# Maxima of the first eight attention units computed between the projections, by sums and differences of key blocks

## The chip, the cores and the metric

The kernel runs on one core of a Trainium2 chip. The metric is the device time of one execution in microseconds (us), lower is better. The core's engines are TensorE (PE, the matmuls), VectorE (DVE), ScalarE (ACT), GpSimd (POOL), and SyncE (SP), whose queue issues the DMAs.

## The reference

One transformer block with adaptive layer norm, all in float32, on 2048 rows of 512 numbers, with 32 heads of 16 and an inner width of 1792:

```python
mod = (silu(c) @ w_mod).reshape(1, 6, 1, 512)
sa, ca, ga, sb, cb, gb = (mod[:, i] for i in range(6))
h = layernorm(x) * (1 + ca) + sa
q, k, v = split(h @ wqkv)                  # 32 heads of 16
p = softmax(q @ k.T / 4)                   # 2048 x 2048 for each head
x = x + ga * ((p @ v) @ wo)
h = layernorm(x) * (1 + cb) + sb
out = x + gb * (gelu(h @ w1 + b1) @ w2 + b2)
```

The softmax needs, for each head and each query row, the largest of 2048 scores before the exponentials are taken.

## The kernel before

The work has three stages: the projections, the attention and the feed-forward part. Products that need more precision than one pass gives are split into a high and a low half, so a product of 512 terms is 12 matmuls of 128x512 (`mm3`, its matmuls on line 274): this is called an item here.

**Projections.** A loop over four blocks `b` of 512 rows normalizes and transposes the block, and computes k and q of the first quarter of the heads (`proj_qk(b, 0, 1)` and `proj_qk(b, 0, 0)`) and four items of v (`proj_v`). Then 24 items follow: k and q of the other three quarters. k and q go to DRAM in their split form (line 297) and are read back in the layout that the attention wants (`build_k`, `build_q`); v goes to DRAM too (line 317) and comes back as `vg` (line 500).

**Attention.** The work is cut into 32 units: a group `g` of four heads (8 groups) times a block `qb` of 512 queries (4 blocks). A unit has 16 steps, one for each 128 keys; there are 512 steps. A step computes four score tiles of 128 keys x 512 queries (`exp_step`: the matmul on line 735 into a bank of the pool `sc`, the exponential by ACT on line 736), named X0 to X3, and one burst P (`pv_step`, line 571), which multiplies the exponentials of the step before with v for the four heads. The four heads of a group lie as two planes `p` and two row halves `a`: heads with a=0 use rows 0 to 49 of PE's array, heads with a=1 rows 64 to 113. So X0 and X2 are in half 0, X1 and X3 in half 1.

**Maxima.** The maxima of a unit are taken before its exponentials and enter the score matmul as two extra rows of the query operand. A unit has 64 banks of them: 128 queries x 512 keys, for 2 planes, 2 halves `a`, 4 query chunks and 4 key blocks (`max_bank`, matmul on line 382). A bank of half 0 is reduced by DVE (line 391). In half 1 two of the four key blocks are reduced like that, and two go by their sum and difference, because max(x, y) = (x+y)/2 + |x-y|/2: the keys' sums and differences were formed in the projections (`pm`, `pmh`, lines 289 to 301, stored as `kpm`), the difference bank goes through |.| on ACT (line 385, in a bank of the pool `sc`), and one DVE instruction (line 388) adds the sum bank and reduces. `max_rows` collects a unit's maxima, transposes them on PE (line 402) and sends them by way of DRAM into the query tile. `next_max(a)` does the next bank of a half; the tokens M0 and M1 stand for it.

The order of a step is written out by hand:

```python
ORDER = ("X0 X1 X2 M1 M0 X3 P".split(), "X0 M1 X1 X2 M1 M0 X3 P M1 M0 M0".split())
```

for even and odd steps: two and six banks, four on average. 83 banks (`LEAD`) are taken ahead, between the matmuls of the last 21 items, four at a time; such a group of banks in an item is called a visit here. PSUM has eight banks: three for maxima (`ps_mx`), four for scores and items (`ps_sc`), one for P (`ps_pv`).

**What sets the order.** Each engine takes its instructions in program order, and a buffer or bank is reused in a ring, so that a matmul that writes a bank waits for the instruction that read it last. SP issues all DMAs in one queue, in order. The hooks (`at`) place side work into steps: output projections of the first query block in the last unit (lines 720 to 725), loads of later groups (lines 741 and 757 to 763).

**Feed-forward.** Line 781 and after; the change does not touch it but for the buffers it inherits.

Of the kernel before, what the change touches and what calls it, by code (L numbers as in the profile page):

```python
# [16 lines left out]
P = 128  # L17
S = 2048
# [16 lines left out]
FILL0 = 3  # L35
LEAD = 2 * NM + 19
# [5 lines left out]
ORDER = ("X0 X1 X2 M1 M0 X3 P".split(), "X0 M1 X1 X2 M1 M0 X3 P M1 M0 M0".split())  # L42
ORDER_END = "X0 X1 P X2 X3".split()
# [4 lines left out]
def block_kernel(ctx: ExitStack, tc: tile.TileContext, x, wqkv, wo, w1, b1, w2, b2, c, w_mod, out):  # L48
# [12 lines left out]
    ps_mx = ctx.enter_context(tc.tile_pool(name="ps_mx", bufs=3, space=PSUM))  # L61
    ps_sc = ctx.enter_context(tc.tile_pool(name="ps_sc", bufs=4, space=PSUM))
    ps_pv = ctx.enter_context(tc.tile_pool(name="ps_pv", bufs=1, space=PSUM))

    def bank_mx():
        return ps_mx.tile([P, TB], F32, tag="mx", name="mx")

    def bank():
        return ps_sc.tile([P, TB], F32, tag="sc", name="sc")

    def bank_pv():
        return ps_pv.tile([P, TB], F32, tag="pv", name="pv")
# [3 lines left out]
    kpm_d = [dram.tile([2, 2, P, TB], F32, name=f"kpm{k}") for k in range(4)]  # L76
# [23 lines left out]
    halves = [[lend.tile([P, 4, D], F32, name=f"{n}{i}") for i in range(2)] for n in ("xin", "wmod")]  # L100

# [6 lines left out]
    c_c = vwpool.tile([P, KC], F32, name="c_c")  # L108
    s_c = vwpool.tile([P, KC], F32, name="s_c")
    s_m = vwpool.tile([P, 2, KC, 32], F32, name="s_m")  # L110
    gp.memset(s_m, 0.0)
    sel = vwpool.tile([P, 32], F32, name="sel")
    sel_b = vwpool.tile([P, 2, P], F32, name="sel_b")
    ones = vwpool.tile([P, 2 * S // P], F32, name="ones")
    gp.memset(ones, 1.0)
    vslots = [vwpool.tile([P, KC, D], FR, name=f"wv{i}") for i in range(2)]
    vraw = vwpool.tile([P, KC, D], F32, name="vraw")
    vst = [vwpool.tile([P, NG, 4, VG], F32, name=f"vst{i}") for i in range(2)]
# [74 lines left out]
    def mod_copy(ps):  # L193
        r = tpool.tile([P, D], F32, tag="h32", name="mrow", bufs=3)
        ac.activation(r, ps, AF.Copy)
        return r
# [61 lines left out]
    def ln1_t(b, tiles, between=lambda: None):  # L258
        hi = hpool.tile([P, KC, TB], FR, name=f"hThi{b}")
        lo = hpool.tile([P, KC, TB], FR, name=f"hTlo{b}")  # L260
        hT[b] = hi, lo
        tr, evac = transposed(tiles, hi, lo, 0, tpool, lambda fc: bank_mx() if fc < KC - 1 else bank(), (ve, gp))
        pss = [tr(fc) for fc in range(KC - 1)]
        between()
        pss.append(tr(KC - 1))
        return lambda: [evac(fc, pss[fc]) for fc in range(KC)]
# [11 lines left out]
    def proj_qk(b, k, w, fill=()):  # L278
# [7 lines left out]
        if w and b == 2:  # L286
            k2[k] = tpool.tile([P, TB], F32, tag="k2", name="k2", bufs=1)
            ac.activation(k2[k], ps, AF.Copy)
        if w and b == 3:
            pm = [tpool.tile([P, TB], F32, tag="h32", name="pm", bufs=3) for _ in range(2)]  # L290
            pmh = [tpool.tile([P, 2, TB], FR, tag="parts", name="pmh", bufs=3) for _ in range(2)]
            for i, op in enumerate((ALU.add, ALU.subtract)):
                ve.tensor_tensor(pm[i], ps, k2[k], op=op)
                ac.activation(pmh[i][:, 0], pm[i], AF.Copy)

        def rest():
            sy.dma_start(qk_d[w][k][:, :, b * TB : (b + 1) * TB].rearrange("a p t -> p a t"), parts.bitcast(F32))
            if w and b == 3:
                for i in range(2):
                    gp.tensor_tensor(pmh[i][:, 1], pm[i], pmh[i][:, 0].bitcast(F32), op=ALU.subtract)  # L300
                    sy.dma_start(kpm_d[k][i].rearrange("a p t -> p a t"), pmh[i].bitcast(F32))
# [3 lines left out]
    def proj_v(b, t):  # L305
# [4 lines left out]
            [w_hi[4][:, i] for i in range(KC)], [w_lo[4][:, i] for i in range(KC)], late_b=False)  # L310
        v = vst[b % 2]
        ac.activation(v[:, :, t, : 4 * VW].rearrange("p g (j e) -> p g j e", e=VW)[:, :, :, :DH],
                      ps.rearrange("p (g j d) -> p g j d", j=4, d=DH), AF.Copy)

    def store_v(b):
        for g in (0, 4):
            sy.dma_start(v_d[g : g + 4, :, b * 4 : b * 4 + 4, :].rearrange("g p k e -> p g k e"),
                         vst[b % 2][:, g : g + 4])
# [3 lines left out]
    kst, kpm, qst = {}, {}, {}  # L322

    def heads(w, g, part, a, t0, t1):
        r0 = (g % 2) * 64
        ap = qk_d[w][g // 2][part, r0 : r0 + 64, t0:t1]
        return ap.rearrange("(p a d) t -> a d p t", a=2, d=DH)[a]

    def build_k(g, t0=0, t1=S):
        for i, part in enumerate((0, 0, 1)):  # L330
            for a in range(2):
                r0 = a * 64 + i * DH
                sy.dma_start(kst[g][r0 : r0 + DH, :, t0:t1].bitcast(F32), heads(1, g, part, a, t0, t1))

    def build_pm(g):

        r0 = (g % 2) * 64
        for i, part in enumerate((0, 0, 1)):
            for w in range(2):
                src = kpm_d[g // 2][w, part, r0 : r0 + 64, :].rearrange("(p a d) t -> a d p t", a=2, d=DH)[1]  # L340
                d0 = 64 + i * DH
                sy.dma_start(kpm[g][d0 : d0 + DH, :, w].bitcast(F32), src)

    def build_q(u):
        g, qb = divmod(u, NB)
        qst[u] = kqpool.tile([P, 2, TB], FR, tag="qst", name="qst", bufs=3)
        for i, part in enumerate((0, 1, 0)):
            for a in range(2):
                r0 = a * 64 + i * DH
                sy.dma_start(qst[u][r0 : r0 + DH].bitcast(F32), heads(0, g, part, a, qb * TB, (qb + 1) * TB))  # L350
# [6 lines left out]
    mx0, mx1, left, vabs = {}, {}, {}, {}  # L357

    mi = [0, 0]

    def max_bank(u, i, a, spare):

        if u not in left:
            mx0[u] = small.tile([P, 2, 4, 4], F32, tag="mx0", name="mx0")
            mx1[u] = small.tile([P, 2, 4, 3], F32, tag="mx1", name="mx1")
            left[u] = 2 * NM
        g = u // NB  # L370
        p, qc, kr = i // 16, (i // 4) % 4, i % 4
        r0 = a * 64
        rows = slice(r0, r0 + KR)
        q = qst[u][rows, p, qc * P : (qc + 1) * P]
        diff, both = a == 1 and kr == 0, a == 1 and kr == 3
        ps = bank() if diff or spare else bank_mx()
        if diff or both:
            k = kpm[g][rows, p, int(diff)]
        else:
            kr -= a  # L380
            k = kst[g][rows, p, kr * TB : (kr + 1) * TB]
        te.matmul(ps, q, k, start=True, stop=True)  # L382
        if diff:
            vabs[u, p, qc] = cpool.tile([P, TB], F32, tag="cp", name="cp")
            ac.activation(vabs[u, p, qc], ps, AF.Abs)  # L385
        elif both:
            v = vabs.pop((u, p, qc))
            ve.tensor_tensor_reduce(v, ps, v, -0.5, 3.0e38, ALU.add, ALU.min, mx1[u][:, p, qc, 2:3])  # L388
        else:
            m = mx1[u][:, p, qc, kr : kr + 1] if a else mx0[u][:, p, qc, kr : kr + 1]  # L390
            ve.tensor_reduce(m, ps, axis=AX.X, op=ALU.max, negate=True)  # L391
        left[u] -= 1

    def max_rows(u):

        mn = small.tile([P, 2, 2, 4], F32, tag="mn", name="mn")
        for a, m in enumerate((mx0.pop(u), mx1.pop(u))):
            ve.tensor_reduce(mn[:, :, a], m, axis=AX.X, op=ALU.min)

        def rest():  # L400
            ps = bank()
# [7 lines left out]
            src = m_d[u].rearrange("s (p a c) q -> a s p (c q)", a=2, c=4)  # L409
            for a in range(2):  # L410
                r0 = a * 64 + KR
                sy.dma_start(qst[u][r0 : r0 + 2].bitcast(F32), src[a])
# [3 lines left out]
    def next_max(a, spare=False):  # L416

        u, i = divmod(mi[a], NM)
        if u == NG * NB:
            return []  # L420
        mi[a] += 1
        max_bank(u, i, a, spare)
# [8 lines left out]
    for t in vst:  # L431
        gp.memset(t[:, :, :, 4 * VW :], 0.0)
        for j in range(4):
            gp.memset(t[:, :, :, j * VW + DH], 1.0)
# [17 lines left out]
    mrow = None  # L452
    for b in range(NB):
        if b == NB - 1:
            close(lcm)
            kqcm, kqpool = pool("kqpool")
            kst[0] = kqpool.tile([P, 2, S], FR, name="kst0")
            kpm[0] = kqpool.tile([P, 2, 2, TB], FR, name="kpm0")
            one_rows(kst[0])
            build_k(0, 0, b * TB)  # L460
            build_q(0)
            build_q(1)
# [9 lines left out]
        if b == NB - 1:  # L472
            build_k(0, b * TB, S)
            build_pm(0)
        if b in (1, 2):
            mrow = mod_rows(wms)
        if b:
            store_v(b - 1)
        proj_v(b, 0)
        if b + 1 < NB:  # L480
            ev = ln1_t(b + 1, xn)
            ev()
        proj_v(b, 1)
# [5 lines left out]
        proj_v(b, 2)  # L489
        proj_v(b, 3)  # L490

    store_v(NB - 1)
    close(vwcm)
    rcm, rpool = pool("rpool", bufs=2)
    cpool = rpool
    vg = {}

    def load_v(g):
        vg[g] = rpool.tile([P, NKC, VG], F32, tag="vg", name="vg")
        sy.dma_start(vg[g], v_d[g])  # L500

    items = [(b, k, w) for k in range(1, 4) for b in range(NB) for w in (1, 0)]
    todo, rest = [], None
    led = 0
    for n, (b, k, w) in enumerate(items):
        if n == 6:
            load_v(0)
        if b == 1 and w and k < 3:
# [3 lines left out]
        fill, new = [], []  # L512
        if rest:
            fill.append(rest)
        m = n + 1 - FILL0

        ms = range(led, min(LEAD, 4 * max(m, 0)))
        fill.append(lambda ms=ms: [new.extend(next_max(i % 2, i % 4 == 3)) for i in ms])
        led += len(ms)
        rest = proj_qk(b, k, w, fill)  # L520
# [3 lines left out]
    rest()  # L524
    close(wcm)
    close(hcm)
    close(tcm)

# [373 lines left out]
```

## Time and profile before

| what | value |
|---|---|
| three runs | 1823.42 us median (1819.85 to 1823.84) |
| the profiled execution | 1823.15 us, its span 1820.9 us |
| granted PE clock, mean | 0.993 |
| loop over b and items of v and first k, q | up to 103.49 us |
| 24 items with 83 banks of maxima, up to the first P | 103.49 to 198.15 us |
| attention, units 0 to 29 | 198.15 to 1379.97 us |
| attention, units 30 and 31 | 36.41 and 41.47 us |
| output projection and feed-forward | 1457.85 to 1820.9 us |

Times inside the execution are counted from the span's start. Busy time of PE is a poor measure of how full it is, since matmuls overlap in the records: one of 512 columns is shown 0.39 to 0.5 us long, while the next one starts 0.23 us after it. So the text below reads starts, not lengths. "PEld" is the loading of the stationary operand. A DMA's line is that of its issue on SP.

### The profile page before, as it was taken

The page shows a single profiled execution, that of the slowest core. Times are in us where ns is not written, and L with a number is a line of the kernel's source. Part 1 is how long each engine was busy: PE and PEld are TensorE (multiplying, and loading weights), DVE is VectorE, ACT ScalarE, POOL GpSimd, SP SyncE. Part 2 cuts the span into 40 slices and gives each one's busy share as a digit, 9 for nine tenths or more (in the row PEclk, how much of TensorE's full clock was granted, in tenths as well). Part 3 has the DMA queues.
Part 4 walks back from the last instruction along what each step waited for, and adds up shares of the span by engine and source line. Part 5 has one row for each costly group of instructions (what it writes and reads, how often), then busy time and mean ns, then how long its engine had stood idle before and what let it go on. Part 6 is the DMA issues. An engine that isn't in the chain of part 4 may idle for free.

```text
span 1820.9 us, 29277 instructions
## 1 busy us (share of the span) xinstructions
PE 1771.5 (97%) x10586; PEld 915.7 (50%) x10586; DVE 1440.5 (79%) x2627; ACT 1337.1 (73%) x2558; POOL 262.1 (14%) x258
## 2 busy tenths in 40 slices
PE   8999999999999999999999999999999999999998
PEld 6776433333333333333333333333333377788887
DVE  6347899989999999998999999899998287737453
ACT  2322799999999999998999999999999732222222
POOL 3111001000000000000000000000002044545462
PEclk8999999999999999999999999999999999999999
DMA  7774611130040122004002100400012054423341
GB/s 254 195 250 180 150 32 28 39 55 14 13 72 14 25 43 43 14 14 72 16 23 51 35 14 14 72 23 16 13 57 83 30 167 140 127 71 109 104 122 47
DMA packets 97960, 129.33 MB, mean 71 GB/s; under 512 B 14152, under 2 KB 53064, under 8 KB 96456
## 3 DMA queue, kind: packets, MB, share of 16 engines
q1 hardware_dynamic: 97816, 127.47, 27.0%
q8 instruction: 83, 1.36, 0.3%
q14 instruction: 61, 0.50, 0.1%
HBM read 91.56 MB, written 35.86 MB: 70 GB/s over the span
## 4 chain that ended last, share of the span: by engine, by line
PE 73%; DVE 15%; DMA 6%; issue 3%; SPq 2%; ACT 1%; POOL 1%; POOLq 0%; DVEq 0%; ACTq 0%
PE pv L571 25%; PE sc L735 12%; PE sc L274 10%; DVE mx L391 10%; PE mx L382 10%; PE mx L802 5%; PE sc L382 5%; DMA kst<-qk 2%; PE pv L802 2%; DMA kpm<-kpm 2%; PE sc L675 1%; DVE cp L388 1%; ACT p L736 1%; DMA qk<-parts 1%; PE mx L675 1%
## 5 line engine op out<-in xcount | busy, mean ns | idle before, releaser
L736 ACT ACTIVATE p<-sc 128x512 f32<-128x512 f32 x2048 | 1060.0, 612 | 58.6 <-PE mx L382 33.3
L391 DVE TENSOR_REDUCE mx<-mx 128x1 f32<-128x512 f32 x1526 | 981.7, 685 | 126.8 <-PE mx L382 94.8
L382 PE MATMUL mx<-kst,qst 48*128 48x512 f32 x1526 | 610.1, 454 | 28.3 <-DVE mx L391 0.4
L735 PE MATMUL sc<-qst,kst 50*128 50x512 f32 x2048 | 633.1, 422 | 1.9 <-ACT p L736 0.9
L571 PE MATMUL pv<-p,vg 128*32 128x512 f32 x4096 | 551.7, 606 | 0.0
L735 PEld LDWEIGHTS sc<-qst,kst 50*128 50x128 f32 x2048 | 309.9, 186 | 233.8 <-ACT p L736 196.3
L382 PEld LDWEIGHTS mx<-kst,qst 48*128 48x128 f32 x1526 | 258.2, 184 | 139.4 <-DVE mx L391 131.9
L781 ACT ACTIVATE g<-sc,b_c 128x512 f32<-128x512 f32 x56 | 38.6, 689 | 240.6 <-PE sc L274 236.5
L385 ACT ACTIVATE cp<-sc 128x512 f32<-128x512 f32 x256 | 153.7, 600 | 34.9 <-PE sc L382 14.4
L388 DVE CUSTOM_DVE_ANT_0 cp<-mx,cp 128x512 f32<-128x512 f32 x246 | 167.5, 681 | 0.3 <-PE sc L735 0.2
L406 POOL CAST m<-mr 16x128 fp32r<-16x128 f32 x32 | 9.1, 286 | 1084.0 <-DVE mr L404 1084.0
L571 PEld LDWEIGHTS pv<-p,vg 128*32 128x32 f32 x4096 | 81.9, 108 | 158.5 <-issue 143.2
L382 PEld LDWEIGHTS sc<-kpm,qst 48*128 48x128 f32 x266 | 48.6, 183 | 208.8 <-ACT p L736 208.8
L785 DVE TENSOR_TENSOR glo<-g,ghi 128x512 fp32r<-128x512 f32 x56 | 59.0, 1054 | 97.2 <-ACT ghi L784 97.1
L382 PE MATMUL sc<-kpm,qst 48*128 48x512 f32 x266 | 131.2, 493 | 2.6 <-DMA qst<-qk 2.6
L607 POOL TENSOR_TENSOR w1l<-w1r,w1h 128x512 fp32r<-128x512 f32 x56 | 76.5, 1366 | 152.7 <-DVE w1h L606 135.1
L382 PE MATMUL mx<-kpm,qst 48*128 48x512 f32 x246 | 97.5, 396 | 0.0
L609 POOL TENSOR_TENSOR w2l<-w2r,w2h 128x512 fp32r<-128x512 f32 x56 | 81.6, 1457 | 6.9 <-DVE w2h L608 6.5
L274 PE MATMUL sc<-p,w1h 128*128 128x512 f32 x224 | 75.0, 396 | 0.0
L274 PE MATMUL sc<-hThi,w 128*128 128x512 f32 x256 | 69.1, 413 | 4.0 <-DVE hThi L242 1.9
L802 PE MATMUL mx<-w2h,glo 128*128 128x512 f32 x168 | 66.2, 394 | 2.7 <-DVE glo L785 2.6
L802 PE MATMUL mx<-w2l,ghi 128*128 128x512 f32 x168 | 65.9, 392 | 0.0
(148 smaller groups left out, 1516.5 us busy)
## 6 DMA issues: line engine op xcount, KB each, us to landing
qk<-parts SPq DMA_DIRECT2D x32, 512.0 KB
w1r<-in_B_w_dram SPq DMA_DIRECT2D x56, 256.0 KB
w2r<-in_B_w_dram SPq DMA_DIRECT2D x56, 256.0 KB
qst<-qk SPq DMA_DIRECT2D x192, 64.0 KB
kst<-qk SPq DMA_DIRECT2D x42, 256.0 KB
wmod<-in_w_mod_dram SPq DMA_DIRECT2D x6, 1024.0 KB
v<-vst SPq DMA_DIRECT2D x8, 664.0 KB
vg<-v SPq DMA_DIRECT2D x8, 664.0 KB
```

What stands on the lines that cost most here:

```text
L274: te.matmul(ps, p, q, start=i == 0, stop=i == len(terms) - 1)
L382: te.matmul(ps, q, k, start=True, stop=True)
L385: ac.activation(vabs[u, p, qc], ps, AF.Abs)
L388: ve.tensor_tensor_reduce(v, ps, v, -0.5, 3.0e38, ALU.add, ALU.min, mx1[u][:, p, qc, 2:3])
L391: ve.tensor_reduce(m, ps, axis=AX.X, op=ALU.max, negate=True)
L571: te.matmul(cur_pv[0][32 * j : 32 * (j + 1)], vg[g][:, kc, j * VW : j * VW + 32], pt.pop((s, j)), start=kc == 0, stop=kc == NKC - 1)
L607: gp.tensor_tensor(alo, a, ahi.bitcast(F32), op=ALU.subtract)
L609: gp.tensor_tensor(blo, b, bhi.bitcast(F32), op=ALU.subtract)
L735: te.matmul(ps, k[r0 : r0 + KX, p, kc * P : (kc + 1) * P], q[r0 : r0 + KX, p], start=True, stop=True)
L736: ac.activation(pb, ps, AF.Exp, scale=SCALE)
L785: ve.tensor_tensor(glo, g, ghi.bitcast(F32), op=ALU.subtract)
L802: te.matmul(acc[qb][t], p[:, sl], q, start=f == 0 and n == 0, stop=f == NF - 1 and n == 2)
```

## The change

All 64 banks of units 0 to 7 (the first two head groups) move between the projections, where four visits of four banks stand in each item (`VISIT`, `FILL0`); each visit holds a pair of difference banks and a pair of sum banks, and a unit's maxima are now all taken by sums and differences of key blocks, block 2r with 2r+1. Sums and differences are formed for the first quarter of the heads alone, now for blocks b=1 and b=3. Eight of the sixteen v items move from the loop over b into the filled part. For that part PSUM is divided into two banks for items and six for maxima, and afterwards as before. What the visits in the items do not hold is done behind the last item.

In the attention, only units 8 to 31 are left: all their banks are plain, with DVE's reduction, and no bank of maxima uses the pool of scores. A step has three banks where it had four, and some steps one more (`EXTRA`). Queries for maxima and for exponentials are loaded into tiles of their own (`qmx`, `qst`), and the keys of a group are loaded a group earlier. The output projections of the first query block are placed in four single steps.

```diff
-FILL0 = 3
-LEAD = 2 * NM + 19
+NU1 = 8
+FILL0 = 2
+VISIT = 2
...
-ORDER = ("X0 X1 X2 M1 M0 X3 P".split(), "X0 M1 X1 X2 M1 M0 X3 P M1 M0 M0".split())
+ORDER = ("X0 X1 M0 X2 M0 X3 P M1".split(), "X0 X1 M1 X2 M1 X3 P M0".split())
+
+EXTRA = {5: 0, 13: 1, 17: 1, 25: 0}
+ORDER_END = "X0 X1 X2 X3 P".split()
...
+    def pair_slot(kind, n):
+        u, i = divmod(n, 16)
...
+        p, qc, r = i // 8, (i // 2) % 4, i % 2
+        t0 = (2 * r + (kind == "V")) * TB
+        pss = [bank_mx() for _ in range(2)]
+        for a, ps in enumerate(pss):
+            rows = slice(a * 64, a * 64 + KR)
+            te.matmul(ps, qmx[u][rows, p, qc * P : (qc + 1) * P], kpm[u // NB][rows, p, t0 : t0 + TB],
+                      start=True, stop=True)
+        if kind == "V" and i == 2:
+            load_qm(u + 1)
+        if kind == "V":
+            for a, ps in enumerate(pss):
+                vabs[n, a] = tpool.tile([P, TB], F32, tag="cp", name="cp", bufs=6)
+                ac.activation(vabs[n, a], ps, AF.Abs)
+            return []
+        for a, ps in enumerate(pss):
+            v = vabs.pop((n, a))
+            ve.tensor_tensor_reduce(v, ps, v, -0.5, 3.0e38, ALU.add, ALU.min, mxs[u][:, p, a, qc, r : r + 1])
...
+    close(acm)
+    open_psum(sc=2, mx=6)
...
+    items = [(None, b, t) for b, t in vitems] + [(k, b, w) for k in range(1, 4) for b in range(NB) for w in (1, 0)]
+    slots = [("V", 0), ("V", 1)]
+    for n in range(2, 16 * NU1):
+        slots += [("V", n), ("U", n - 2)]
+    slots += [("U", 16 * NU1 - n) for n in (2, 1)]
...
+    def visit():
+        nonlocal led
+        for sl in slots[led : led + VISIT]:
+            new.extend(pair_slot(*sl))
+        led += VISIT
...
+        if n >= FILL0:
+            fill = [lambda rest=rest: (rest(), visit()), visit, visit, visit]
+        rest = proj_qk(b, k, w, fill) if k else proj_v(b, w, fill)
...
     rest()
+    while led < len(slots):
+        new = []
+        visit()
+        todo += new
...
+    open_psum(mx=3, sc=4, pv=1)
...
+    for t, n in enumerate((base - 2, base + 3, base + 7, base + 11)):
         for i in range(12):
-            at(base + OP0 + (12 * t + i) // OPN, lambda t=t, i=i: run(("o", t), lambda: o_proj(0, t), i))
...
+            at(n, lambda t=t, i=i: run(("o", t), lambda: o_proj(0, t), i))
...
-        if kc == 2 and u + 2 < NU:
-            build_q(u + 2)
+        if kc == 2 and 0 < u < NU - 1:
+            load_q(u + 1)
...
+        order = ORDER[s % 2] + [f"M{a}" for k, a in EXTRA.items() if k % 16 == kc and (k < 16 or u < 4)]
...
-            if g:
-                kst[g + 1] = kst[g - 1]
-                build_k(g + 1)
-                kpm[g + 1] = kpm[g - 1]
-                build_pm(g + 1)
+            if g and g + 3 < NG:
+                load_k(g + 3, kst[g - 1])
```

287 lines of the change are left out of this document (151 added, 136 removed).

## The prediction

> **What bounds the kernel now.** I read the busy shares first, then the timeline of TensorE (PE) in two attention steps, then the same in the projections. The busy shares name a candidate and no more:
>
> ```profile
> span 1820.9 us, 29277 instructions
> ...
> PE 1771.5 (97%) x10586; PEld 915.7 (50%) x10586; DVE 1440.5 (79%) x2627; ACT 1337.1 (73%) x2558; POOL 262.1 (14%) x258
> ```
>
> The timeline (start, length, engine, line, tile, count) shows what a step is made of. Between two bursts of P·V (L571) stand matmuls on 48 or 50 rows: the exp scores (L735) and the maxima (L382). They use one half of the array's rows each, a=0 or a=1, as the code sets.
>
> ```profile
> 801.14 0.49 PE L735 MATMUL sc<-qst,kst 50*128 50x512 f32 x1
> 801.15 0.49 PE L382 MATMUL mx<-kst,qst 48*128 48x512 f32 x1
> 801.48 0.39 PE L735 MATMUL sc<-qst,kst 50*128 50x512 f32 x2
> 801.71 0.39 PE L382 MATMUL mx<-kpm,qst 48*128 48x512 f32 x1
> 801.71 0.40 PE L382 MATMUL mx<-kst,qst 48*128 48x512 f32 x1
> 801.95 0.40 PE L735 MATMUL sc<-qst,kst 50*128 50x512 f32 x1
> 802.27 1.07 PE L571 MATMUL pv<-p,vg 128*32 128x512 f32 x8
> 803.27 0.50 PE L382 MATMUL sc<-kpm,qst 48*128 48x512 f32 x1
> 803.27 0.73 PE L382 MATMUL mx<-kst,qst 48*128 48x512 f32 x2
> 803.62 0.63 PE L735 MATMUL sc<-qst,kst 50*128 50x512 f32 x2
> 803.85 0.44 PE L382 MATMUL mx<-kst,qst 48*128 48x512 f32 x1
> 804.09 0.39 PE L735 MATMUL sc<-qst,kst 50*128 50x512 f32 x1
> 804.59 0.49 PE L382 MATMUL mx<-kst,qst 48*128 48x512 f32 x1
> 804.59 0.49 PE L735 MATMUL sc<-qst,kst 50*128 50x512 f32 x1
> 805.01 1.06 PE L571 MATMUL pv<-p,vg 128*32 128x512 f32 x8
> ```
>
> Matmuls of different halves start together (801.14 and 801.15); those of one half follow each other. So an interval between bursts costs **slots**: as many as the fuller half has matmuls. The first slot lasts 0.34 us (801.14 to 801.48), a later one 0.234, the last 0.326 up to the burst (801.95 to 802.27), the burst 1.00 (802.27 to 803.27). The first interval has four slots: 0.34+2x0.234+0.326+1.00 = 2.13. The second has five in half a=0 (M0 M0 X0 X2 M0): 2.37 by the same sum, but takes 2.74, since its last M0 waits until 804.59. The waits name VectorE (DVE): the ring of maxima has three banks, four M fall into this interval, and the fourth needs the first one's reduction (start 803.85, 0.69 long). The pair is 4.87 us, a unit of 16 steps about 39.2. DVE works 7 x 0.60 of those 4.87 us, ScalarE (ACT) 8 exps at 0.478 and one Abs at 0.49: neither fills it.
>
> The projections, as items of 12 full matmuls (L274), without and with one visit of four maxima banks:
>
> ```profile
> 103.49 1.98 PE L274 MATMUL sc<-hThi,w 128*128 128x512 f32 x8
> ...
> 106.21 1.98 PE L274 MATMUL sc<-hThi,w 128*128 128x512 f32 x8
> ...
> 128.63 0.73 PE L382 MATMUL mx<-kst,qst 48*128 48x512 f32 x3
> ...
> 129.30 2.10 PE L274 MATMUL sc<-hThi,w 128*128 128x512 f32 x8
> 131.24 1.07 PE L274 MATMUL sc<-hTlo,w 128*128 128x512 f32 x4
> 132.23 0.50 PE L382 MATMUL mx<-kst,qst 48*128 48x512 f32 x1
> ```
>
> An item without a visit is 106.21-103.49 = 2.72 us. From visit to visit it is 132.23-128.63 = 3.60. **A visit costs 0.88 us**: two slots and the change of shape before and after them. Here too PE is the bound.
>
> **The change, part by part.** Own time 1823.15 us (span 1820.9 and 2.25 around it; 0.27 under the median 1823.42, so the forecast stands for the median too).
>
> *Visits added between the projections.* 512 banks (units 0 to 7) stand there in place of 83. That is 128 visits of four; items 2 to 31 take four each, 120, and eight are left behind the last item. An item becomes 2.72+4x0.885 = 6.26 us, 30 of them 187.8, and the two before them 5.44. DVE has 8 combined maxima at 0.605 (802.32 to 802.92 in the trace) and one 0.6 subtraction in it, 5.4 us; ACT 8 Abs and a copy at 0.49, 4.4. Both hide under 6.26; if ACT or DVE lags at the split of weights (two 0.63 copies), that is some tenths per item, at most 12 us over all.
>
> *The rest behind the items.* Eight visits have no full matmul beside them; there DVE sets the pace, 16x0.605 = 9.7, and then the first two steps up to the first burst, some 4.3 (before, 6.0 passed from the last visit at 192.17 to the first burst at 198.15, pair sums and a clock of 0.57 included): 14, within 11 to 17.
>
> *The first visit.* It comes 2 items and three matmuls, 6.1 us, after the last projection of k=0. It needs sums, differences and queries by way of DRAM. Before, 22 us lay between. The chain now, from rows of before: copy and subtraction, two sums, two splits and two GpSimd subtractions of 1.3, store, about 3 us to landing, then 12 loads at 0.5 to 0.6 of issue on SP's in-order queue and 2 to landing: some 14 us. PE waits about 8, within 0 and 15. Everything in PE's queue stands behind that wait, the next full matmuls too.
>
> *V items moved.* Four of them (10.9 us) leave the loop over b for the filled part; they have been counted above. They covered the next block's transposes and splits, and block 1 gets a set of sums on DVE, ACT and POOL that it did not have. I put 3 us back, within 0 and 8. The loop then ends at 92.61-10.9+3 = 84.7. The v stores become 16 of half the size and the q loads double; DMA share is 0.18 in attention, so I give them nothing.
>
> Sum up to the first burst: 84.7+5.4+8+187.8+14 = 299.9 against 198.15: **+101.8**.
>
> *Attention, units 0 to 29* (198.15 to 1379.97, 1181.8 us). Each interval has four X and three M, and three banks serve three M: the wait at 804.59 goes, and what is late next is the slots. Even step: M0 X0 M0 X2 M0 in half 0, two X in half 1. Odd step: M1 X1 M1 M1 X3 in half 1, two X in half 0. **Five slots in both**: 0.34+3x0.234+0.326+1.00 = 2.37, where before five and four alternated. DVE needs 3x0.60 and ACT 4x0.478 of it, and every bank is free a step ahead. 480x2.367 = 1136.2. The 68 extra banks bring the fourth M back into one interval each: 0.26 and a slower restart of 0.1 (between 0 and 0.6): 24.5. Transposes of 23 maxima rows at 0.21 (the step of 2.34 in each unit): 4.8. Sum 1165.5, **-16.3**; in it are some 6 us of waits at changes of key group that I let go, since the next keys now come a group earlier. Fewer Abs and reductions give nothing: they were not what a step ended on.
>
> *Units 30 and 31.* The maxima run out at step 8 of unit 30. Steps without them take 1.94 (as the last six of unit 30 do now); an output projection in one step makes it 1.67+12x0.227+0.66 = 5.05. Unit 30: 9x2.37+0.6+7x1.94+3.4 = 38.9 (36.4 now). Unit 31: 13x1.94+3x5.05 = 40.4 (41.5 now). **+1.4.** The FFN (363 us) is unchanged.
>
> Total 1823.15+101.8-16.3+1.4 = **1910 us**.
>
> **Rivals.** *Attention gains more than the projections lose* (faster). Break-even needs steps of (1181.8-101.8-1.4)/480 = 2.25 us, extras included, so 2.19 without: fewer than 4.3 slots where I count five. Were five matmuls of one half to run in the time of four, 480x0.234 = 112 us go: 1798. For it: X1 may be taken before X0 when its half is free, so the order is not rigid. Against it: 803.62, 803.85 and 804.09 are 0.234 apart, half 0 being full each time. [...]
>
> *Visits cheaper.* If a denser mix of shapes paid only the slots, 2x0.234, 120x0.417 = 50 us go: 1860. Every visit in the trace paid 0.88.
>
> *Evacuation becomes the bound between the projections.* A combined maximum needs its difference's Abs two slots earlier and shares six banks and six buffers with it. If the two did not overlap, a visit would take 2x0.49+2x0.605 = 2.2 and not 1.56 with its three full matmuls: +76, 1986. Against it: DVE fills 5.4 of 6.26. [...]
>
> *The change does less than it says:* sums and differences halve DVE's passes for eight units, but DVE was hidden; that lies in the forecast.
>
> **How the numbers follow.** Forecast 0.80, faster rival 0.06, cheap visits 0.06, evacuation 0.06, a wash 0.02. All low ends together (no first wait -8, loop -3, rest -3, attention -29, tail -5) give 1862; all high ends (+7, +5, +3, lags +12, attention +17, tail +3) 1957. They will not all fall together; 1866 to 1944 leaves out the two outer rivals and a little of the forecast. Faster by over 0.2% (what a measurement of this kernel can tell from no change) 0.07, within it 0.01, slower 0.92.
>
> **What would show it.** Items between the projections 6.2 to 6.3 us apart, PE without gaps in them; a PE gap of about 8 us after the second item; first burst near 300 us; attention steps 2.37 in both parities, 2.7 where an extra bank stands. It is wrong if steps are near 2.13, if items exceed 6.6, or if a visit costs under 0.7.

## The result and the profile after

The changed kernel takes **1945.68 us** (median of four runs, 1940.8 to 1953.68), the kernel before 1821.63 (1818.51 to 1823.84): a ratio of 1.0687, 95% interval [1.0641, 1.0732]. It is slower, as forecast, by 124 us instead of 87; the forecast of 1910 and the upper end of its range, 1944, are both too low. The profiled execution is 1953.68 us with a span of 1951.9, 131.0 more than the span before; the sums below are made on the two spans. Where one run of a kernel lies over 1.5% above its fastest (one run each of experiments 3 and 4), its median leaves that run out.

The page of the changed kernel (busy shares, and the granted clock of TensorE in 40 slices of 48.8 us):

```profile
PE 1908.6 (98%) x10586; PEld 988.4 (51%) x10586; DVE 1444.5 (74%) x2591; ACT 1345.3 (69%) x2552; POOL 256.3 (13%) x259
...
PEclk9979996699999999999999999999999999999999
```

PE's share hardly differs from before (97%), and DVE's and ACT's busy time neither. The row that does differ is the last: two slices at 0.6 and one at 0.7, in the stretch from the projections into the attention. PE is "busy" there at half speed, so its share cannot show it. The windows of the changed kernel (stretch, length, then busy time of PE, PEld, DVE, ACT and POOL with counts, granted clock, DMA share, GB/s) put a place to it:

```profile
102.00:123.00 21.00, 10.69 (x28) 5.45 (x28) 3.76 (x11) 5.80 (x11) 0.00 (x0) 0.51 1.09 153
...
307.00:323.00 16.00, 13.15 (x41) 6.77 (x40) 13.95 (x43) 10.30 (x19) 1.42 (x4) 0.50 0.20 56
323.00:386.40 63.40, 63.40 (x248) 25.59 (x248) 33.57 (x52) 33.41 (x65) 0.00 (x0) 0.56 0.47 63
386.40:1516.90 1130.50, 1127.18 (x7048) 477.63 (x7047) 927.24 (x1511) 969.81 (x1887) 37.18 (x62) 1.00 0.17 35
```

Between 102 and 123 us PE is busy for half of the time and at half the clock; the DMA engines are full (a share of 1.09) at only 153 GB/s. The first unit of attention (323.0 to 386.4) takes 63.4 us; PE is busy throughout, at a clock of 0.56. The other 29 units of the forecast's stretch run at 1.00. The timeline of PE shows what stands ahead of these stretches (in brackets: PE's idle time before the group, and what ended it):

```profile
71.85 1.93 PE L201 MATMUL sc<-wmod,s_m 128*32 128x512 f32 x8 [5.57 <-DMA wmod<-in_w_mod_dram]
...
91.95 2.03 PE L290 MATMUL sc<-wv,hThi 128*128 128x512 f32 x8
...
112.31 1.33 PE L414 MATMUL mx<-kt,qmx 48*128 48x512 f32 x4 [10.98 <-DMA qmx<-qk]
...
115.15 1.22 PE L414 MATMUL mx<-kt,qmx 48*128 48x512 f32 x4
...
126.23 0.73 PE L414 MATMUL mx<-kt,qmx 48*128 48x512 f32 x4
```

At 71.85 PE has waited for the loads of `w_mod`. The last projection of k=0 ends at 91.95, where the next item starts. The first visit (L414) starts at 112.31 after a wait of 11 us, and at first a visit of four banks is shown 1.22 long (115.15); from 123 us on the same group takes 0.73 (126.23). Behind the last item:

```profile
304.75 11.00 PE L414 MATMUL mx<-kt,qmx 48*128 48x512 f32 x32
318.16 0.38 PE L436 MATMUL mx<-ident,mn 128*16 128x128 f32 x1 [2.41 <-DVE mn L432]
...
323.00 1.93 PE L635 MATMUL pv<-p,vg 128*32 128x512 f32 x8
...
327.30 1.93 PE L635 MATMUL pv<-p,vg 128*32 128x512 f32 x8
```

The 32 banks behind the items run at the pace of the reductions, then PE waits 2.41 us for the last maxima. From 307.1 to 378.8 us the granted clock is half: a burst takes 1.9 us and a step 4.29 (323.00 to 327.30). The fall at 307.1 stands 8.6 us ahead of the wait of 2.41 us, so that wait did not set it off; what stands ahead of it is the thin stretch from 304.75 on, eight matmuls in 2.4 us where four take 0.66 ahead of it; the trace shows PE busy in it. At step 12 of the unit the full clock returns, and steps are 2.35 to 2.37 in both parities from there on, 2.71 with an extra bank. One of them:

```profile
500.74 1.06 PE L635 MATMUL pv<-p,vg 128*32 128x512 f32 x8
501.74 0.50 PE L397 MATMUL mx<-kt,qmx 48*128 48x512 f32 x1
501.74 0.83 PE L802 MATMUL sc<-qst,kt 50*128 50x512 f32 x3
502.31 0.39 PE L397 MATMUL mx<-kt,qmx 48*128 48x512 f32 x1
502.54 0.39 PE L802 MATMUL sc<-qst,kt 50*128 50x512 f32 x1
502.78 0.39 PE L397 MATMUL mx<-kt,qmx 48*128 48x512 f32 x1
503.09 1.07 PE L635 MATMUL pv<-p,vg 128*32 128x512 f32 x8
```

Five slots follow each other: the first at 501.74, the second within the group of three, then 502.31, 502.54 and 502.78, and the burst at 503.09.

Where the 131.0 us lie, against the forecast:

| stretch | before | after | change | forecast |
|---|---|---|---|---|
| start to first P | 198.15 | 323.00 | +124.85 | +101.8 |
| units 0 to 29 | 1181.82 | 1193.91 | +12.09 | -16.3 |
| units 30, 31 to the start of the last P | 79.90 | 77.30 | -2.60 | +1.4 |
| from there to the end | 361.03 | 357.69 | -3.34 | 0 |

### The profile page after: what moved, and what is told of

Read it like the earlier page. It is cut to its first block, busy times and chain, and to the rows that moved or that the text cites. A ratio compares the mean times of both kernels' runs of the same rounds, so it can differ in the third digit from the quotient of the medians.

```text
span 1951.9 us, 29242 instructions
## 1 busy us (share of the span) xinstructions
PE 1908.6 (98%) x10586; PEld 988.4 (51%) x10586; DVE 1444.5 (74%) x2591; ACT 1345.3 (69%) x2552; POOL 256.3 (13%) x259
## 4 chain that ended last, share of the span: by engine, by line
PE 88%; DVE 5%; DMA 4%; issue 2%; POOL 1%; ACT 0%; SPq 0%; DVEq 0%; POOLq 0%; ACTq 0%
PE pv L635 26%; PE mx L397 22%; PE sc L802 14%; PE sc L290 12%; PE mx L867 5%; PE mx L414 4%; PE pv L867 2%; PE sc L742 1%; DVE mxs L399 1%; DMA wmod<-in_w_mod_dram 1%; DMA kt<-kpm 1%; DMA rb<-rden 1%; DMA kpm<-pmh 1%; PE mx L742 1%; DVE cp L425 0%
## 5 line engine op out<-in xcount | busy, mean ns | idle before, releaser
L399 DVE TENSOR_REDUCE mxs<-mx 128x1 f32<-128x512 f32 x1536 | 968.9, 684 | 235.5 <-PE sc L802 169.3
L802 PE MATMUL sc<-qst,kq 50*128 50x512 f32 x1024 | 315.0, 448 | 0.4 <-DVE mr L438 0.4
L397 PE MATMUL mx<-kt,qmx 48*128 48x512 f32 x768 | 312.3, 449 | 1.4
L397 PE MATMUL mx<-kq,qmx 48*128 48x512 f32 x768 | 305.3, 434 | 2.0 <-DVE mxs L399 0.8
L802 PE MATMUL sc<-qst,kt 50*128 50x512 f32 x1024 | 304.9, 430 | 0.0
L397 PEld LDWEIGHTS mx<-kt,qmx 48*128 48x128 f32 x768 | 143.2, 193 | 251.6 <-DVE mxs L399 207.6
L397 PEld LDWEIGHTS mx<-kq,qmx 48*128 48x128 f32 x768 | 138.4, 185 | 244.5 <-DVE mxs L399 218.1
L421 ACT ACTIVATE cp<-mx 128x512 f32<-128x512 f32 x256 | 140.3, 597 | 57.5 <-PE mx L414 55.3
L802 PEld LDWEIGHTS sc<-qst,kq 50*128 50x128 f32 x1024 | 147.3, 192 | 37.2 <-ACT p L803 21.4
L802 PEld LDWEIGHTS sc<-qst,kt 50*128 50x128 f32 x1024 | 142.7, 185 | 14.2
L414 PE MATMUL mx<-kt,qmx 48*128 48x512 f32 x512 | 102.7, 472 | 11.2 <-DMA qmx<-qk 11.0
L414 PEld LDWEIGHTS mx<-kt,qmx 48*128 48x128 f32 x512 | 43.9, 192 | 62.9 <-issue 23.7
```

The source lines that it names most:

```text
L397: te.matmul(ps, qmx[u][rows, p, qc * P : (qc + 1) * P], kst[u // NB][rows, p, kr * TB : (kr + 1) * TB], start=True, stop=True)
L399: ve.tensor_reduce(mxs[u][:, p, a, qc, kr : kr + 1], ps, axis=AX.X, op=ALU.max, negate=True)
L414: te.matmul(ps, qmx[u][rows, p, qc * P : (qc + 1) * P], kpm[u // NB][rows, p, t0 : t0 + TB], start=True, stop=True)
L421: ac.activation(vabs[n, a], ps, AF.Abs)
L802: te.matmul(ps, k[r0 : r0 + KX, p, kc * P : (kc + 1) * P], q[r0 : r0 + KX, p], start=True, stop=True)
```

## The experiments

The theory after the result: the slots and visits are as forecast, and the missing 44 us are waits of PE that the change brought, the half clock that PE runs at around and behind them, and a dearer transposition of the maxima rows. The rivals: the emptying of the banks sets the pace, or the steps are long because of the ring of three banks and not because of slots. All times are medians; "plain step" is one without an extra bank or transposition.

**1. Keep PE busy behind the items.** The changed kernel, with small identity matmuls added between the visits that stand behind the last item:

```diff
...
     while led < len(slots):
...
         visit()
+        spin(2)
         todo += new
+    spin(8)
     for f in todo:
         f()
+    spin(4)
```

> The changed kernel, with small matmuls on the identity (two behind each visit, eight and four more) put behind the last item, where PE otherwise idles while DVE catches up. Theory (slots and clock): what the forecast missed is mostly PE's clock, which falls to half after PE has waited, and PE waits behind the last item; with PE kept occupied the first unit falls from 63.4 us to about 39.5, the clock shows no half rate after 300 us, and the time falls by 24 to 32 us to 1912 to 1922. Rival: the first unit's own thin use of the array (one half for three slots of five) or its loads bring the half clock, whatever stands before it; then the first unit stays near 63 us and the time at 1941 to 1954.

1930.45 us, ratio 1.0594 [1.0564, 1.0623]. The windows behind the items and of unit 0:

```profile
307.00:324.30 17.30, 16.91 (x100) 11.52 (x98) 15.20 (x46) 10.43 (x21) 1.45 (x4) 1.00 0.15 45
324.30:363.40 39.10, 38.94 (x245) 16.59 (x244) 32.23 (x53) 33.35 (x67) 0.00 (x0) 1.00 0.77 105
```

The clock is 1.00 from 125.8 us on, behind the items too, and unit 0 takes 39.1 us instead of 63.4, with the same instructions of attention. So the 24 us of unit 0 are the clock, and the clock there depends on what PE does in the 16 us before it. The profiled executions differ by 24.1 us, the medians by 15: below the 24 to 32 that were expected. The profiled execution of the changed kernel is its slowest, with a mean clock of 0.972; the other three have 0.974, 0.978 and 0.978, so the half clock does not last equally long in every execution.

**2. Mix the halves.** One M of each half in the place of two of the same:

```diff
-ORDER = ("X0 X1 M0 X2 M0 X3 P M1".split(), "X0 X1 M1 X2 M1 X3 P M0".split())
+ORDER = ("X0 X1 M1 X2 M0 X3 P M0".split(), "X0 X1 M1 X2 M0 X3 P M1".split())
```

> The changed kernel with one line of another order: even steps X0 X1 M1 X2 M0 X3 P M0, odd steps X0 X1 M1 X2 M0 X3 P M1; as many banks of each half, but 4 and 3 matmuls on the two halves in each interval in place of 5 and 2. Theory (slots): each plain step takes 0.34+2x0.234+0.326+1.00 = 2.13 us in place of 2.36, units 35 in place of 38.5 to 39, the time falls by 100 to 120 us to 1825 to 1845. Rival (the step is paced by ACT's exponentials, by DVE or by the ring of banks): steps stay at 2.3 or more and the time above 1925.

1852.71 us, 1.017 [1.0137, 1.0204]: 93 us less than the changed kernel, for four tokens of the order, and short of the 100 to 120 that were expected. The timeline of PE in one step of this kernel:

```profile
802.16 1.07 PE L635 MATMUL pv<-p,vg 128*32 128x512 f32 x8
803.16 0.50 PE L397 MATMUL mx<-kq,qmx 48*128 48x512 f32 x1
803.16 0.77 PE L802 MATMUL sc<-qst,kq 50*128 50x512 f32 x3
803.74 0.44 PE L397 MATMUL mx<-kq,qmx 48*128 48x512 f32 x2
...
804.36 1.07 PE L635 MATMUL pv<-p,vg 128*32 128x512 f32 x8
```

An interval still holds seven short matmuls, four X and three M, but no half has more than four: bursts at 802.16 and 804.36 are 2.20 apart and the steps alternate between 2.12 and 2.19, where five slots took 2.36. The forecast's four-slot price was 2.13. The ring of three banks and DVE are the same in both kernels, so the slot count is what makes a step of the changed kernel long. Not all of the 93 us are slots: in the profiled executions units 1 to 29, at full clock but for 3.4 us, fall from 1130.5 to 1052.2 us (-78), and unit 0 falls from 63.4 to 39.4, mostly because its half clock happened to end 49 us sooner. The steps with an extra bank stayed at 2.71.

**3. Three pairs a visit, three visits an item.** The same number of banks with fewer changes of shape:

```diff
-VISIT = 2
+VISIT = 3
...
-            fill = [lambda rest=rest: (rest(), visit()), visit, visit, visit]
+            fill = [lambda rest=rest: (rest(), visit()), visit, visit]
```

> The changed kernel with three visits of three pairs in an item in place of four visits of two pairs. Theory: a visit's price is 0.234 for each pair and 0.42 for its two changes of shape, so a visit of three pairs costs 1.12, an item 2.72+3x1.12 = 6.08 us with nine pairs in it and not eight; nothing is left behind the last item, so PE does not wait there, and the first unit runs at full clock: 1945 falls by 40 to 50 us. Rival: the price is 0.22 for each bank, whatever the shape; then an item takes 2.72+18x0.22 = 6.7 us, and only the clock's part (24 us) goes.

1975.63 us (three runs, 1956.59 to 1985.68; a fourth took 1990.36), 1.0823 [1.0743, 1.0903]: 30 us more than the changed kernel where 40 to 50 less were expected. The expectation fell: from 180 to 300 us an item takes 8.0 us, not 6.08. The timeline of PE, and one row of the waits between 180 and 320 us (sum, times, longest), say why:

```profile
204.04 0.96 PE L414 MATMUL mx<-kt,qmx 48*128 48x512 f32 x6
...
206.75 1.72 PE L414 MATMUL mx<-kt,qmx 48*128 48x512 f32 x5 [0.20 <-ACT cp L421]
```

```profile
ACT cp L421 <- DVE mxf L425: 30.4, 33, 1.6
```

An undisturbed visit of six banks takes 0.90 on PE (204.04 to the next full matmul at 204.94) against 0.66 for four: one more slot of 0.234, as the slots say. But the next one stops after one bank, and its other five start at 206.75. Its six banks are the whole ring: ACT's copy waits for a buffer that DVE has not yet read (30.4 us in sum), and PE's weight loads wait for ACT in turn (22.3). So the evacuation of the banks is the bound with three pairs a visit; with two it is not (the same wait of PE for ACT is 1.9 us in the changed kernel, 130 to 300 us). Half clock, 349.8 to 411.2 us, followed here too: unit 0 took 65.1.

**4. Loads earlier.** The load of the first queries ahead of the last block's projections, and those of `w_mod` one step earlier:

```diff
             build_k(kts[0], kpm_d, 0, 0, 2 * TB)
+            load_qm(0)
...
-            load_qm(0)
...
             mrow = mod_rows(wms)
+            if b == 1:
+                wms = [load_wm(2, 0), load_wm(5, 1)]
...
-            wms = [load_wm(2, 0), load_wm(5, 1)]
```

> The changed kernel with two loads issued earlier: the second pair of w_mod right behind the matmuls that read the first, and the first queries for maxima ahead of the last block's projections. Theory: the waits of PE in the loop over b (5.6 us on w_mod) and before the first visit (11 us) are set by the place of these loads in SP's queue; the first wait shrinks by 4 to 6 us, the other by 3 to 6, and the half clock after them shortens: 10 to 16 us. Rival: the DMA engines are full there whatever the order, and under 3 us are won.

1927.61 us (three runs, 1923.82 to 1946.79; a fourth took 1996.95), 1.0604 [1.0535, 1.0673]. The loop over b ends at 85.17, 6.8 us sooner and within 0.5 of the forecast's 84.7. The first visit did not follow:

```profile
95.38 1.65 PE L290 MATMUL sc<-wv,hThi 128*128 128x512 f32 x3 [4.44 <-ACT vst L330]
...
104.39 1.61 PE L414 MATMUL mx<-kt,qmx 48*128 48x512 f32 x2 [6.63 <-DMA kt<-kpm]
```

Its second pair needs the sums of blocks 2 and 3, which come last. The wait named in the changed kernel (the queries) had hidden this one. The expectation was half right, and the 18 us that were won are in the main luck: in the profiled execution the first P comes only 4.9 us sooner, while unit 0 takes 42.0 us in place of 63.4, since the half clock behind the items happened to last 20.5 us and not 71.7.

**5. Early loads and first key pair first.** In addition, the visits take all slots of key blocks 0 and 1 before those of 2 and 3, and the ring of split projections gets a fourth buffer:

```diff
-        p, qc, r = i // 8, (i // 2) % 4, i % 2
+        p, qc, r = (i // 4) % 2, i % 4, i // 8
...
-        parts = tpool.tile([P, 2, TB], FR, tag="parts", name="parts", bufs=3)
+        parts = tpool.tile([P, 2, TB], FR, tag="parts", name="parts", bufs=4)
```

> The changed kernel with the waits ahead of and at the first visit taken away at their cause: the two early loads of the run before, the key blocks of a unit in the order first pair of blocks, then second (so the first eight pairs of slots need only what block 1 stored), and four buffers in place of three for the split projections (ACT's copy of the last one waited for a store to land). Theory (waits and the clock after them): the first visit comes 6 to 9 us after the last item of k=0 and not 20, PE shows no half clock between 90 and 125 us, the first P comes near 297 us (323 now); the half clock behind the last item stays, of varying length; 1905 to 1930 in all. Rival: the DMA engines are full there, the first visit comes at 15 us or later and the first P after 312.

1930.16 us, 1.0608 [1.0575, 1.064]. The first visit starts at 88.23 after a wait of 1.49 us, as expected, but half clock follows it here too (89.2 to 96.0). At 126.64 PE has waited again, 6.09 us, and from the middle of that wait on the clock is half (123.3 to 137.0); first P at 308.7 instead of 297. A wait taken away at one place came back at another.

**6. All of it.** Experiments 1, 2 and 5 together, with two extra banks a unit in place of the list of the changed kernel:

```diff
-EXTRA = {5: 0, 13: 1, 17: 1, 25: 0}
+EXTRA = {5: 0, 13: 1}
```

> All at once: the kernel of the run before, the small matmuls behind the last item, the mixed order of halves, and two extra banks a unit and no more (62, not 70). Theory: the parts add up, -26 for the first visit, -24 and the rest of the clock behind the last item, -95 for the steps, -4 for the extras: 1795 to 1815, the first P near 298 with no half clock after 30 us, plain steps 2.13 to 2.19. Rival: with one wait gone another takes its place (steps fall onto ACT or DVE, the evacuation in the visits), 1830 or more.

1832.32 us, 1.0073 [1.0052, 1.0094], above the 1795 to 1815 that were expected and as the rival said: one wait gone, another in its place. The second wait remains; PE, and SP's queue in the same kernel:

```profile
132.24 1.28 PE L414 MATMUL mx<-kt,qmx 48*128 48x512 f32 x2 [4.29 <-ACT cp L421]
```

```profile
107.83 8.30 SPq L347 DMA_DIRECT2D kt<-kpm  x6
116.23 15.86 SPq L332 DMA_DIRECT2D v<-vst  x4
```

The engine named, ACT, is not the cause. ACT's own longest wait there is 7.4 us, at the copy of a v item for a buffer whose store has not landed; its copies of maxima stand behind that copy in its queue. The store stands in SP's queue behind six issues of the second group's keys (8.30 us for them).

**7. Extra banks in the score pool.** Experiment 6, with the fourth M of a step in a bank of the score pool:

```diff
...
-        ps = bank_mx()
+        ps = bank() if spare else bank_mx()
...
```

> The kernel of the run before with the extra bank of a step taken from the pool of scores in place of the ring of three. Theory: a step with an extra bank takes 2.7 us because the fourth bank waits for the first one's reduction; from another pool it takes 2.2 to 2.35, 62 x 0.4 = 25 us less than the run before. Rival: the wait moves to a score matmul, which now needs that bank, and the step keeps its 2.6 or more; within 8 us of the run before.

1845.46 us, 1.0135 [1.0105, 1.0165]: 13 us more where 25 less were expected. A step with an extra bank takes 2.84 to 2.87 instead of 2.71. The fourth user of three maxima banks is cheaper than the fifth of four score banks.

**8. The kernel before, with mixed halves.** Its 64 banks a unit in four a step, spread so that no half has more than four slots, with a spare one in the score pool:

```diff
-ORDER = ("X0 X1 X2 M1 M0 X3 P".split(), "X0 M1 X1 X2 M1 M0 X3 P M1 M0 M0".split())
+ORDER = ("X0 X1 X2 M1 M0 X3 P M0".split(), "X0 M1 X1 X2 M1 S0 X3 P M1 M0".split())
...
-                new += next_max(int(tok[1]))
+                new += next_max(int(tok[1]), tok[0] == "S")
```

> The kernel BEFORE with one line of another order and nothing of the change between the projections: even steps X0 X1 X2 M1 M0 X3 P M0, odd steps X0 M1 X1 X2 M1 S0 X3 P M1 M0, where S0 is a bank of half 0 in the pool of scores. Each interval has four matmuls on each half, three banks of the ring and one of the pool of scores. Theory (slots and the ring): both intervals have four slots and no wait for a bank; DVE has 7 x 0.60 = 4.2 and ACT 4.32 us in two steps, so two steps take 4.3 to 4.5 in place of 4.87, and the time falls by 90 to 130 us to 1690 to 1730. Rival: DVE and ACT are so full that each wait costs; two steps take 4.7 or more, the time above 1785.

1965.14 us, 1.0798 [1.0771, 1.0826]: steps of 2.60 and 2.84 where before had 2.13 and 2.74. The expectation fell:

```profile
903.45 0.40 PE L382 MATMUL sc<-kst,qst 48*128 48x512 f32 x1
904.15 0.50 PE L735 MATMUL sc<-qst,kst 50*128 50x512 f32 x1 [0.30 <-ACT p L736]
```

The last exponential's matmul stands at 904.15, 0.70 after the spare bank at 903.45 instead of 0.234, waiting for ACT to free a score bank. So slots alone don't set a step: it is slots, as long as three M and four X fit their rings. In this order the kernel before, with four M a step, could not use its four slots; the changed kernel's three M a step can. No other order of the kernel before was run.

**9. Keys of the second group later.** Experiment 6, with the second group's keys loaded after the v items, and ten identity matmuls ahead of the first visit:

```diff
-        if n == 3:
+        if n == nv + 4:
             build_k(kts[1], kpm_d, 1)
...
     def visit():
         nonlocal led
+        if led == 0:
+            spin(10, bank_mx())
```

> The kernel with all the parts (extras in the ring of three) with two edits more: the load of the second group's key sums, which stood in front of four stores of v in SP's queue and is not needed for 100 us, is issued eight items later, and ten small matmuls stand ahead of the first visit. Theory: in the run before, PE waited 2 us at the first visit and 5 us at 127 us (ACT held up by a store of v behind that load), each followed by 14 us at half clock; both go, 8 to 20 us: 1812 to 1824, the first P near 300 us. Rival: the DMA engines stay full until 133 us, another store or load is late in its place, and under 5 us are won.

1818.36 us (11 runs), 0.9982 [0.9971, 0.9993]. The first P:

```profile
301.31 1.06 PE L646 MATMUL pv<-p,vg 128*32 128x512 f32 x8
```

That is within 1.4 us of the forecast's 299.9, partly by luck: the first visit waits 2.3 us for the added identity matmuls in place of 8 for loads, and the rest behind the items, with identity matmuls in it, takes 18.6 in place of 14. Units 0 to 29 take 1080.9 us, so 2.252 a step. The forecast put break-even at 2.25, and the two kernels are level there.

**10. The transposition in the score pool.** Experiment 9, with the transposition of the 16 maxima rows in a bank of the score pool, where the kernel before has it:

```diff
-            ps = bank_mx()
+            ps = bank_mx() if u < NU1 else bank()
```

> The kernel of the run before with one bank moved: the transpose of a unit's maxima in the attention goes through the pool of scores, as in the kernel before the change, and not through the ring of three. Theory: a step with this transpose takes 0.58 us more in the ring of three (it is the fourth user in its interval) and took 0.21 in the pool of scores; 24 units x 0.37 = 9 us less, 1806 to 1812. Rival: a score matmul waits in its place (as the extra banks in the pool of scores did), and it stays within 3 us of the run before.

1828.08 us, 1.0033 [1.0017, 1.0049]: the step with the transposition went from 2.70 to 3.24, an exponential's matmul waiting for ACT behind it:

```profile
480.37 0.28 PE L436 MATMUL sc<-ident,mn 128*16 128x128 f32 x1
...
481.76 0.49 PE L813 MATMUL sc<-qst,kt 50*128 50x512 f32 x1 [0.22 <-ACT p L814]
```

That it is the ring of maxima alone that makes it dear has fallen.

**11 and 12. The transposition right behind the burst**, in the ring of maxima and in the score pool. Experiment 9 and the following lines, in 12 with the line of experiment 10 besides:

```diff
                     pv_step(s - 1)
+                for f in todo[:1]:
+                    f()
+                todo = todo[1:]
             else:
                 new += next_max(int(tok[1]))
-        for f in todo[:1]:
-            f()
-        todo = todo[1:] + new
+        todo = todo + new
```

> The version with all edits and late keys, with one more: the transposition of a unit's 16 maxima is issued right behind the burst P instead of behind the bank of maxima that follows P. There it costs 0.52 to 0.59 us per unit, since the step is 2.70 instead of 2.12 or 2.19. Theory of place: a full-array matmul directly behind the burst pays no change of shape, as in the kernel before (0.21 us there), and the slot that M lost by standing alone (0.43 to the transposition) comes back. The step becomes 2.3 to 2.4, 24 of them save 8 us: 1808 to 1812 us. Rival, the ring of three banks: the transposition takes the free bank, M behind it waits for one more reduction (about 0.4), everything behind M with it: step 2.55 to 2.7, saving 0 to 3 us: 1815 to 1819.

> As the version with the transposition right behind the burst, with its bank taken from the score pool, as it was in the kernel before. Theory of place alone: step 2.3 to 2.4, 1808 to 1812 us. Rival, the fifth user of four score banks: an exponential's matmul waits for ScalarE, step 2.8 or more, as 3.24 with the score pool behind M: 1820 to 1828 us. If the ring decides in the other version and this one shows 2.3 to 2.4, the price of the transposition is the ring's and not the place's.

1811.3 us, 0.9955 [0.9937, 0.9973], and 1816.04 us, 0.9971 [0.9956, 0.9986]. The step is 2.32 to 2.35 in the ring; in the score pool it is 2.32 to 2.34 but for six units with 2.40 to 2.53, and in both 2.9 where it falls on an extra bank. PE in experiment 9, and then in 11:

```profile
484.32 0.50 PE L397 MATMUL mx<-kq,qmx 48*128 48x512 f32 x1
484.75 0.28 PE L436 MATMUL mx<-ident,mn 128*16 128x128 f32 x1
484.96 0.72 PE L813 MATMUL sc<-qst,kt 50*128 50x512 f32 x3
```

```profile
487.38 1.07 PE L646 MATMUL pv<-p,vg 128*32 128x512 f32 x8
488.38 0.28 PE L436 MATMUL mx<-ident,mn 128*16 128x128 f32 x1
488.58 0.50 PE L397 MATMUL mx<-kq,qmx 48*128 48x512 f32 x1
```

Behind M the transposition is a full-height matmul between two of 48 rows: M stands alone for 0.43 (484.32 to 484.75), the transposition takes 0.21, and only then do the exponentials start. Right behind the burst it takes 0.20 and nothing else, and M follows at once. The theory of place held: with the pool the same, place alone takes the step from 2.70 to 2.33 (9 and 11) and from 3.24 to 2.33 (10 and 12). Experiment 11 is 0.45% faster than the kernel before, with an interval clear of 1.

## Why the prediction was right in direction and short in amount

**The loop over b** failed: "I put 3 us back" and an end at 84.7; it was 91.95 (+7.3). The v items also covered the loads of `w_mod`: PE waits 5.57 and 0.74 us for them and runs at half clock from 71.6 to 78.4. Experiment 4, loading them earlier, has its end at 85.17.

**The first visit** failed: "PE waits about 8"; from 91.95 plus the 6.1 us of work it is 14.3 (+6.3), just inside the range 0 to 15 that was given for it. The chain's length is not what was wrong: it is the order of transfers behind it. "I give them nothing", of the v stores and the q loads, rested on the DMA share of the attention (0.18), where the stage they stand in has 1.09. Experiments 4, 5, 6 and 9 took the waits apart one after the other: queries, sums of the second key pair, v stores behind keys in SP's queue.

**Visits and items** held: an item mostly takes 6.2 to 6.3 us at full clock against 6.26, (6.2-2.72)/4 = 0.87 a visit. Up to 122.8 us they ran at half clock, which cost some 5 us. **The rest behind the items** failed: 18.5 instead of 14, 11.0 for the 32 banks (9.7), and 7.5 (4.3) for the chain of the last maxima and the first steps, at half clock. The four terms, 7.25, 6.26, 5.09 and 4.46, make +23.1, all of the miss up to the first P.

**Attention** held in its steps (2.36 against 2.37 in both parities, 2.71 with an extra bank against 2.73), and its sum failed by 28.4. Unit 0 at half clock is +24 of it (experiment 1). "Transposes at 0.21" was the second: they cost 0.58 in most units and 0.40 in five, 12.4 us and not 4.8, since in the new order they stand behind an M (experiments 9 to 12). Plain steps a little below the forecast's give most of the remaining 4 back.

**Units 30 and 31** were off by 4 us, half of it because the marker "1457.85" taken for the end of unit 31 was not the start of the last P, which stands at 1459.87. The part behind it, given nothing, took 3.3 us less; why is not shown.

The step that failed most is thus none of the terms of work but one that has no term: the forecast saw a PE gap of 8 us and a chain behind the items, and priced what PE waits there, not the clock that it runs at. It gave all 480 steps the full clock; the first 16 took 63.4 us, where 39.1 is what they take at full clock. The 0.57 that it did count was from a stretch of 3.4 us. Of the 44 us missed, 24 (unit 0) are shown to be that; some 5 (first items) and part of the rest are read from the trace.

**The rivals.** Cheaper visits: no. Evacuation as the bound: no with two pairs a visit, yes with three (experiment 3). The faster rival asked for five matmuls of a half in the time of four: no, the spacing at full clock stayed at 0.23 us (501.74 to 503.09 above). Its argument, that the order is not rigid, holds: in that interval, which the program writes as M X X M X M X, three X and one M have started by 502.10. But what starts ahead is in the half that has two, and the other has its five all the same. The rival's step is reachable by other means, though: four slots, 2.12 and 2.19 us. The forecast saw that break-even lay below 4.3 slots and did not look at whether three M and four X could be dealt as four and three.

What is open: what ends a stretch of half clock. It lasted 71.7 us in the changed kernel, 61.4 in experiment 3, 44.4 in 5, 20.5 in 2 and in 4, behind the same items, with PE busy on the steps of attention from the first P on (in 2 on the mixed ones). No run here varies that by itself. Open too is what exactly brings the fall at 307.1: experiment 1 fills the thin stretch and the wait behind it at once.

## What to carry to other kernels

Where TensorE is the bound, price a wait or a thin stretch twice: what it lasts, and the clock that comes with it; here 28 small matmuls without use kept the full clock and took 15 us off. Count short matmuls by the half of the array that they use, deal them evenly over the halves (2.12 and 2.19 us a step with four in the fuller half, 2.36 with five), and put full-height ones next to other full-height ones (a transposition: 0.20 us behind a burst, 0.58 behind an M). When a wait is removed, ask at once what is next in the same queue: in experiments 5 and 6 the engine that was named was not the one that was late.

## What the runs showed of the hardware

**Half clock after a short wait or a thin stretch, for long.** Ahead of the last 3 us of the span, the stretches of half clock are 6.8, 6.8, 20.5 and 71.7 us in the changed kernel (2, 2, 6 and 21 times 3.41), and 3.4 at the shortest in the kernel before (855.0 to 858.4). In experiment 12 PE waited for a reduction in the middle of attention:

```profile
1370.23 0.49 PE L397 MATMUL mx<-kq,qmx 48*128 48x512 f32 x1 [0.84 <-DVE mxs L399]
```

```profile
1372.40:1382.60 10.20, 10.20 (x45) 3.88 (x37) 5.77 (x11) 5.56 (x11) 2.50 (x2) 0.50 0.01 2
```

From 1372.4 to 1382.6 us the clock was half, PE being busy for all 10.2 us, and unit 29 took 42.1 us where it takes 36.3 in experiment 11. That is about 6 us. The profiled execution of 11 has 3.0 of that kind in unit 0; without both, units 0 to 29 are alike within 0.5 us in the two. Whether that is the distance of their medians is not shown. This fall and that of the changed kernel at 307.1 had no long wait ahead of them: PE was busy for 9.47 of the 10.4 us ahead of 1372.4, its longest wait 0.84, and for 26.97 of the 27.0 us ahead of 307.0. Nor did a busy PE soon end the half clock: of the 71.7 us from 307.1 on, PE was busy for all of the last 55.8.

**Small packets.** The v stores became 16384 packets of 332 bytes (median 21 ns each) in place of 4096 of 1328 bytes (61 ns): 16 bytes a ns instead of 22. The key loads in packets of 4096 and 8192 bytes took 491 and 1062 ns, some 8 bytes a ns, where packets of 2048 bytes took 84 ns, 24 bytes a ns. In the window of 102 to 123 us, with its DMA share of 1.09 at 153 GB/s, the two kinds took 241 of the 367 us of packet time; most of the rest are packets of 2048 bytes, at a median of 200 ns there.
